# Layer 1 beside attention in halves of a product, row sums joined with 1e-9 by a reduce, and one raw-weight buffer given up for one more gated output

## The chip, the cores and the metric

One Trainium2 chip, one core of it. The metric is the device time of the kernel in microseconds (us), lower is better. The core has five engines that run side by side: PE (TensorE, with its weight loads shown as PEld), DVE (VectorE), ACT (ScalarE), POOL (GpSimd) and SP (SyncE, which here only issues transfers). Each runs its own list of instructions in order and waits on semaphores of the others.

## The reference

Attention with a mask by blocks of 64, for 4 batches, 8 heads, 576 positions and 64 features, then two feed-forward layers over 2304 tokens (512 features, 2048 hidden). All in float32.

```python
scores = scale * q @ k.T                       # 576 x 576 a head
scores = where(block_i >= block_j, scores, -1e9)
attn = exp(scores - max); attn /= attn.sum(-1) + 1e-9
x = (attn @ v) as 2304 x 512
h = x @ w_in;  g = max(h, 0) + alpha * min(h, 0);  x = g @ w_out        # layer 1
h = x @ w_in2; g = where(h > 0, h, exp(min(h, 0)) - 1); out = g @ w_out2  # layer 2
```

## The kernel before

**Precision.** Matrix products run in a reduced float32 with each factor split into a high and a low part, three products for one (`PASSES`). So whatever PE multiplies is first split on another engine: `copy` (L82 to L90) makes the high part, `low_part` (L78) the rest. Weights arrive as raw 64-bit floats, 512 KB a piece, and are turned into words and then split by `load_w` (L110): a transfer into a raw buffer (`wraw`, 3 buffers), two ACT operations (L127, L128), three DVE operations (L132, L133, L137), a POOL add (L142), an ACT copy (L151) and a DVE subtraction (L83, into `w`). A raw buffer is in use from the issue of its transfer until the POOL add. There are 64 such pieces, 32 a layer.

**Attention** goes by slots. A slot scores one tile of rows of a pair of heads. The first 16 slots (EARLY) are the first 256 rows of each of the 16 pairs; then come three slots a pair, i = 2, 3, 4. In a slot PE makes scores into one of two score buffers in PSUM (`twin`, ring `s`), DVE masks by memset (L299, L304) and takes the maximum (L296), ACT takes the exponential with its row sum (L324), two slots later DVE adds 1e-9 (L329) and inverts (L330) the sum and POOL scales the rows (L90), then PE transposes them (L352 to L369), and later multiplies by v (L413). Since two score buffers alternate, scores of a slot wait for the exponentials of the slot two before. Splits of q and k for later pairs (`split_q`, `split_k`) lie mostly on POOL.

**Layer 1 beside attention.** With only hidden units 0 to 511 (`FA` = 4 tiles of 128), layer 1 is computed for three units of 512 tokens as soon as their attention rows exist (`l1_beside`). A unit has 8 parts: four products into hidden tiles (L536, 12 matmuls of 512 columns each, then a gate on ACT, DVE, ACT and POOL) and four products into partial outputs (L557, 12 matmuls, then a copy to `z` that goes to DRAM). A loop in the main program puts a part on PE, then some slots, then a part. All parts use one PSUM bank (ring `h` is bank 7 alone). The order of every engine up to here is that of the code.

**The rest** (from 301 us on) runs steps: a hidden tile of a unit (12 matmuls), then two steps later the output of it (12 matmuls, L628 in layer 1, L603 in layer 2). Units A, B and D are layer 1, C is layer 2; A is 16 steps, 8 with 512 tokens and 8 with 256, B is three units of 4 steps. Here only PE's order is the code's; the other engines' lists, SP's too, are put in order ahead of time by a scheduler that works with its own estimates. It may start transfers and splits of weights long before their step, as soon as a raw buffer is free in its plan. Outputs of gates go to `gs_tile` (4 buffers `gs`, 3 buffers `gsl`).

## Time and profile before

| what | value |
|---|---|
| median of 3 runs | 1059.77 us (1059.53 to 1062.9) |
| the profiled execution | 1062.1 us, its span 1060.0 us |
| PE busy | 983.2 us, 93% of the span |
| DVE busy | 579.2 us, 55% |
| ACT, POOL busy | 442.8 us (42%), 358.7 us (34%) |
| mean granted clock of PE | 0.975 of 2.4 GHz |

The span is counted from the first to the last instruction; 2.1 us of the profiled execution lie outside of it. The busy shares are means over stretches that differ: beside attention all four compute engines are in use, in the last third PE alone is full.

### The profile page before, as it was taken

Reading aid. Unit: us, or ns where it says so; the run is one execution under the profiler, and the core shown is the slowest. Engines: PE = TensorE matmul, PEld = TensorE weight load, DVE = VectorE, ACT = ScalarE, POOL = GpSimd, SP = SyncE. Lnnn points to the kernel's source line nnn. Section 1 sums busy time; section 2 is a strip of 40 time slices with the busy share of each in tenths; the row PEclk is TensorE's granted clock in tenths of the full one; section 3 lists DMA queues with packets and bytes.
Section 4 is the critical chain, followed back from the end, with each engine's and each line's share of the span. In section 5 each row is a group of like instructions: output and inputs, shape, how many; then the busy total and the mean of one; then the engine's idle time right before and its main releaser. Section 6 shows DMA issues by size and latency. Waiting matters only on the chain.

```text
span 1060.0 us, 14175 instructions
## 1 busy us (share of the span) xinstructions
PE 983.2 (93%) x5072; PEld 790.7 (75%) x5072; DVE 579.2 (55%) x1047; ACT 442.8 (42%) x986; POOL 358.7 (34%) x410
## 2 busy tenths in 40 slices
PE   4888988998798799999999998899999999999997
PEld 3555765666577677878988887688888888888897
DVE  6886587677648995483313189833333333333343
ACT  4675566666635663353323255422222222222222
POOL 6876566667426663353323254200000000000000
PEclk9888999999999899999999999899999999999999
DMA  6451533353544767563526255200200300110010
GB/s 185 135 183 41 194 110 115 103 171 97 172 150 145 252 235 240 160 205 112 167 75 197 81 179 218 80 1 10 110 0 1 119 1 1 40 41 1 1 40 20
DMA packets 61157, 116.27 MB, mean 110 GB/s; under 512 B 11552, under 2 KB 29984, under 8 KB 59936
## 3 DMA queue, kind: packets, MB, share of 16 engines
q1 hardware_dynamic: 60800, 115.11, 32.8%
q8 instruction: 40, 0.66, 0.3%
q14 instruction: 29, 0.24, 0.1%
q10 hardware_dynamic: 288, 0.26, 0.1%
HBM read 83.89 MB, written 31.46 MB: 109 GB/s over the span
## 4 chain that ended last, share of the span: by engine, by line
PE 66%; DVE 16%; issue 5%; DMA 4%; POOL 4%; ACT 3%; SPq 1%; POOLq 0%; DVEq 0%; ACTq 0%
PE bank L603 18%; PE bank L578 18%; PE bank L536 10%; PE bank L628 9%; PE bank L413 4%; DVE w L83 4%; DVE wword L137 3%; DMA wraw<-w 3%; PE bank L557 2%; DVE wword L133 2%; DVE wword L132 2%; PE bank L359 2%; PE pair L279 2%; POOL p L90 1%; POOL wword L142 1%
## 5 line engine op out<-in xcount | busy, mean ns | idle before, releaser
L536 PE MATMUL bank<-x,w 128*128 128x512 f32 (+1 forms) x960 | 216.3, 376 | 2.2 <-DVE xtail L83 1.3
L578 PE MATMUL bank<-x,w 128*128 128x512 f32 (+1 forms) x960 | 211.4, 369 | 0.0
L536 PEld LDWEIGHTS bank<-x,w 128*128 128x128 f32 x960 | 171.1, 193 | 33.6 <-ACT xtail L419 1.4
L578 PEld LDWEIGHTS bank<-x,w 128*128 128x128 f32 x960 | 170.4, 190 | 31.7
L583 DVE TENSOR_SCALAR e<-e 128x512 f32<-128x512 f32 (+1 forms) x80 | 33.1, 414 | 181.3 <-ACT e L582 181.3
L603 PE MATMUL bank<-w,gs 128*128 128x512 f32 x498 | 123.1, 394 | 3.1 <-DVE z L639 2.1
L582 ACT ACTIVATE e<-bank 128x512 f32<-128x512 f32 (+1 forms) x80 | 44.4, 554 | 194.3 <-PE bank L578 194.3
L519 DVE SCALAR_TENSOR_TENSOR g<-neg,beta,bank 128x512 f32<-128x512 f32 (+1 forms) x80 | 55.1, 689 | 117.6 <-ACT neg L516 117.6
L142 POOL TENSOR_TENSOR wword<-wword,wraw 128x512 int32<-128x512 int32 x64 | 88.8, 1389 | 81.3 <-DVE wword L137 30.2
L603 PEld LDWEIGHTS bank<-w,gs 128*128 128x128 f32 x498 | 93.3, 189 | 23.8 <-DVE z L639 3.2
L628 PE MATMUL bank<-gs,w 128*128 128x512 f32 (+1 forms) x480 | 105.0, 366 | 4.8 <-POOL gs L83 2.6
L83 POOL TENSOR_TENSOR gs<-g,gs 128x512 fp32r<-128x512 f32 (+1 forms) x52 | 65.2, 1253 | 118.4 <-ACT gs L523 118.1
L628 PEld LDWEIGHTS bank<-gs,w 128*128 128x128 f32 x480 | 83.4, 190 | 20.7 <-POOL gs L83 3.4
L90 POOL TENSOR_SCALAR p<-p,stat 128x128 f32<-128x128 f32 (+4 forms) x144 | 84.2, 599 | 42.5 <-DVE stat L330 26.5
L324 ACT ACTIVATE p<-pair,stat 128x128 f32<-128x128 f32 (+4 forms) x144 | 78.2, 555 | 34.3 <-DVE stat L296 33.9
L603 PE MATMUL bank<-w,gsl 128*128 128x512 f32 x366 | 88.7, 390 | 0.0
L628 PE MATMUL bank<-gsl,w 128*128 128x512 f32 (+1 forms) x336 | 77.1, 377 | 11.1 <-POOL gsl L83 6.6
L516 ACT ACTIVATE neg<-bank 128x512 f32<-128x512 f32 (+1 forms) x80 | 44.0, 550 | 95.0 <-PE bank L536 94.9
L603 PEld LDWEIGHTS bank<-w,gsl 128*128 128x128 f32 x366 | 68.3, 188 | 13.8
L628 PEld LDWEIGHTS bank<-gsl,w 128*128 128x128 f32 x336 | 59.8, 193 | 24.3 <-POOL gsl L83 7.9
L83 DVE TENSOR_TENSOR w<-wword,w 128x512 fp32r<-128x512 f32 x64 | 68.7, 1091 | 14.2 <-ACT w L151 13.7
L296 DVE TENSOR_REDUCE stat<-pair 128x2 f32<-128x256 f32 (+3 forms) x80 | 63.1, 805 | 6.9 <-PE pair L285 4.8
(81 smaller groups left out, 1277.2 us busy)
## 6 DMA issues: line engine op xcount, KB each, us to landing
wraw<-w SPq DMA_DIRECT2D x64, 512.0 KB, 4.4
x<-xd SPq DMA_DIRECT2D x24, 512.0 KB, 7.4
xd<-x SPq DMA_DIRECT2D x4, 2048.0 KB, 6.7
x<-yd SPq DMA_DIRECT2D x4, 2048.0 KB, 8.0
vraw<-v_a SPq DMA_DIRECT2D x24, 256.0 KB, 4.5
zd<-z SPq DMA_DIRECT2D x20, 256.0 KB, 3.4
kraw<-kT SPq DMA_DIRECT2D x16, 288.0 KB, 3.2
yd<-gs SPq DMA_DIRECT2D x8, 512.0 KB, 4.9
```

Source lines behind the costliest of these rows:

```text
L83: return {"v": dve, "p": pool_e}[eng].tensor_tensor(out=out, in0=x, in1=f32(high), op=ALU.subtract)
L90: return pool_e.tensor_scalar(out, x, 1.0 if scale is None else scale, 1.0, ALU.mult, ALU.mult)
L142: pool_e.tensor_tensor(out=w, in0=w, in1=units, op=ALU.add)
L296: peak = lambda out, x, axis=AX.X: dve.tensor_reduce(out=out, in_=x, axis=axis, op=ALU.max, negate=True)
L324: act.activation(out=out, in_=x, func=AF.Exp, bias=stat[:, k:k + 1], accum_out=stat[:, w + k:w + k + 1])
L516: act.activation(out=neg, in_=h, func=AF.Relu, scale=-1.0)
L519: dve.scalar_tensor_tensor(out=g, in0=neg, scalar=beta[:, f:f + 1], in1=h, op0=ALU.mult, op1=ALU.add)
L536: pe.matmul(h, w_in(0, f, wp_, kc), x[:, xp_, kc, :n], start=kc == 0 and t == 0, stop=kc == KC - 1 and t == 2)
L578: pe.matmul(h, w_in(1, f, wp_, kc), x[:, xp_, kc, :], start=kc == 0 and t == 0, stop=kc == KC - 1 and t == 2)
L582: act.activation(out=e, in_=h, func=AF.Exp)
L603: pe.matmul(acc, gs[:, gp_, tg * P:(tg + 1) * P], w_out(1, f, wp_, 0, DM), start=f == 0 and t == 0, stop=f == NF - 1 and t == 2)
L628: pe.matmul(acc, w_out(0, f, wp_, m * P, P), gs[:, gp_, :n], start=first and t == 0, stop=last and t == 2)
```

## The change

Six edits:
- `l1_beside` puts half a product (6 matmuls) on PE at a time, 16 parts a unit instead of 8, over the same slots (10 for unit 0, 24 for units 1 and 2). The rule that deals out the slots is the same: after each part, the slots left over the parts left, rounded up.
- The high part of every early q goes to ACT instead of POOL (7 operations; the first one was on ACT before).
- The two masks of an early slot are one memset.
- Row sums go to every second column of a `stat` tile whose other columns hold 1e-9; the sum with 1e-9 is a DVE reduce over pairs instead of an add (`tensor_scalar`), and the inverse is taken in place. The six `stat` tiles are fixed and set once on POOL at the start.
- Two raw-weight buffers (and two word buffers) instead of three.
- Gated outputs alternate between 4 `gs` and 4 `gsl` buffers, instead of 4 and 3.

```diff
-    wraw_p = ctx.enter_context(pool("wraw", 3))
+    wraw_p = ctx.enter_context(pool("wraw", 2))
...
-            copy("a" if c.start == 0 and n == 0 else "p", qh, q[:, c], 0.125)
+            copy("a" if c.start == 0 else "p", qh, q[:, c], 0.125)
...
+    stats = [ap1.tile([P, 16], F32, name=f"stat{i}") for i in range(6)]
+    for t in stats:
+        pool_e.memset(t, 1e-9)
...
-            for t, lo, hi in EARLY_TILES:
-                dve.memset(sb[:64, :, hi - 64:hi], NEG)
+            dve.memset(sb[:64].rearrange("p x (t c) -> p x t c", t=2)[:, :, :, 64:P], NEG)
...
-        dve.tensor_scalar(stat[:, 2 * w:3 * w], stat[:, w:2 * w], 1e-9, None, ALU.add)
-        dve.reciprocal(stat[:, 3 * w:4 * w], stat[:, 2 * w:3 * w])
+        total = stat[:, TOTALS:TOTALS + w]
+        dve.tensor_reduce(out=total, in_=stat[:, SUMS:SUMS + 2 * w].rearrange("p (k t) -> p k t", t=2),
+                          axis=AX.X, op=ALU.add)
+        dve.reciprocal(total, total)
...
-        if late_pools and turn[0] % 7 % 2:
-            return late_pools[0].tile([P, 2, 512], F32R, tag="gsl", name="gsl", bufs=3)
+        if late_pools and turn[0] % 2:
+            return late_pools[0].tile([P, 2, 512], F32R, tag="gsl", name="gsl", bufs=4)
...
         for f in range(FA):
-            h = l1_h(u, f)
-            gs[f] = l1_gate(f, h, n, True)
-            end_tick()
-            yield
+            h = bank[take("h")][:, :n]
+            for part in halves:
+                for kc in part:
+                    for t, (wp_, xp_) in enumerate(PASSES):
+                        pe.matmul(h, w_in(0, f, wp_, kc), x[:, xp_, kc, :n],
+                                  start=kc == 0 and t == 0, stop=kc == KC - 1 and t == 2)
+                if part is halves[1]:
+                    gs[f] = l1_gate(f, h, n, True)
+                    end_tick()
+                yield
...
-            parts, n = l1_beside(u), FA + KC
+            parts, n = l1_beside(u), 2 * (FA + KC)
```

Three places show what this does to the lists.

PE, units 1 and 2 beside attention. Before, one cycle of three slots (`L279` 128x512 is the score of i = 3, `L285` of i = 4, `L279` 128x384 of i = 2 of the next pair; `p` rows are transposes, `vraw` rows the products with v):

```order
L536 MATMUL bank_106<-x_869,w 128x512 x12
L279 MATMUL pair_101<-kh,qh 128x512 x2
...
L365 MATMUL bank_104<-ident,p_1294 128x128 x4
...
L285 MATMUL pair_102<-kh,qdiag_117 128x288
...
L359 MATMUL bank_104<-ident,p_1345 128x128 x3
L279 MATMUL pair_101<-kh,qh 128x384 x2
...
L413 MATMUL bank_105<-pt,vraw_114 64x320 x6
...
L359 MATMUL bank_104<-ident,p_1388 128x128 x4
L536 MATMUL bank_106<-x_869,w 128x512 x12
```

The same engine, the cycle after the change:

```order
L562 MATMUL bank_106<-x_838,w 128x512 x6
L279 MATMUL pair_102<-kh,qh 128x512 x2
...
L373 MATMUL bank_105<-ident,p_1378 128x128 x4
...
L285 MATMUL pair_101<-kh,qdiag_115 128x288
...
L367 MATMUL bank_105<-ident,p_1444 128x128 x3
L562 MATMUL bank_106<-x_838,w 128x512 x6
L279 MATMUL pair_102<-kh,qh 128x384 x2
```

Six of twelve matmuls stay where the twelve were, and six now stand ahead of the scores of i = 2. In this part of a unit (its first 16 slots) six matmuls come every two slots, in the last 8 slots of a unit every slot.

PE, the end of unit 0, after the change:

```order
L573 MATMUL bank_106<-gs,w 128x512 x6
L279 MATMUL pair_101<-kh,qh 128x384 x2
...
L367 MATMUL bank_105<-ident,p_1077 128x128 x4
L573 MATMUL bank_106<-gs,w 128x512 x36
L562 MATMUL bank_106<-x_838,w 128x512 x6
```

Unit 0 has 10 slots for 16 parts, so its last six parts follow each other with no slot between; before, each part had one or two slots behind it.

DVE, unit A (gates are `g<-neg,beta,bank`, the rest are weights). Before, from the fourth gate to the fifth:

```order
L519 SCALAR_TENSOR_TENSOR g<-neg,beta,bank_3229 128x512
L83 TENSOR_TENSOR w<-wword,w 128x512 x3
L132 TENSOR_SCALAR wword<-wword 128x512
L133 TENSOR_SCALAR wword<-wword 128x512
L137 SCALAR_TENSOR_TENSOR wword<-wraw,wword 128x512
L132 TENSOR_SCALAR wword<-wword 128x512
L519 SCALAR_TENSOR_TENSOR g<-neg,beta,bank_3230 128x512
```

After:

```order
L527 SCALAR_TENSOR_TENSOR g<-neg,beta,bank_3161 128x512
L132 TENSOR_SCALAR wword<-wword 128x512
L133 TENSOR_SCALAR wword<-wword 128x512
L137 SCALAR_TENSOR_TENSOR wword<-wraw,wword 128x512
L83 TENSOR_TENSOR w<-wword,w 128x512
L527 SCALAR_TENSOR_TENSOR g<-neg,beta,bank_3162 128x512
```

Seven weight operations between two gates have become four here; over the first 18 gates (the 16 of A and two of B) there were 87, and there are 66. The other 21 stand later in the list, among the gates of B and D.

SP, unit A (`L117` is a raw weight piece, `x<-xd` the input of the next unit, for B's three units in turn). Before:

```order
L117 DMA wraw<-w 128x1024 x9
L501 DMA x_3556<-xd_83 128x2x512 x4
L117 DMA wraw<-w 128x1024 x3
...
L117 DMA wraw<-w 128x1024 x6
L501 DMA x_3879<-xd_84 128x2x512 x4
```

After:

```order
L117 DMA wraw<-w 128x1024 x8
L509 DMA x_3488<-xd_83 128x2x512 x4
L117 DMA wraw<-w 128x1024 x2
...
L117 DMA wraw<-w 128x1024 x4
L509 DMA x_3811<-xd_84 128x2x512 x4
```

The input of B's second unit stands behind 14 weight pieces where it stood behind 18.

## Rows read from the trace of the kernel before

**Rows 1.** Busy time by stage: engine busy (instructions), granted clock, DMA share, GB/s.

```profile
0.00:58.00 58.00, 37.73 (x275) 26.93 (x276) 44.48 (x108) 35.04 (x123) 44.26 (x75) 0.94 0.51 156
58.00:118.00 60.00, 51.80 (x293) 37.22 (x294) 40.38 (x95) 34.47 (x104) 39.24 (x62) 0.89 0.40 143
118.00:301.40 183.40, 159.40 (x1052) 112.58 (x1050) 130.77 (x300) 114.67 (x298) 110.72 (x152) 0.96 0.42 130
301.40:402.00 100.60, 88.80 (x453) 75.20 (x454) 87.69 (x116) 59.20 (x111) 56.52 (x40) 0.95 0.58 199
...
640.00:690.00 50.00, 44.16 (x177) 34.22 (x176) 43.55 (x59) 23.92 (x42) 18.87 (x13) 0.93 0.39 147
```

**Rows 2.** Groups by shape, 0 to 110 us: busy, mean ns, idle before.

```profile
L329 DVE TENSOR_SCALAR stat<-stat 128x4 f32<-128x4 f32 x16 | 7.2, 452 | 0.0
L296 DVE TENSOR_REDUCE stat<-pair 128x2 f32<-128x256 f32 x16 | 6.8, 424 | 0.5
...
L299 DVE MEMSET pair<- 64x128 f32 x32 | 5.3, 165 | 1.8
...
L90 POOL TENSOR_SCALAR qh<-qraw 128x512 fp32r<-128x512 f32 x7 | 4.7, 678 | 4.5 <-DMA qraw<-qT 3.9 <-PE pair L279 0.6
...
L89 DVE COPY z<-bank 128x512 f32<-128x512 f32 x1 | 0.7, 692 | 2.1 <-PE bank L557 2.1
...
L87 ACT ACTIVATE qh<-qraw 128x512 fp32r<-128x512 f32 x1 | 0.6, 629 | 1.2 <-DMA qraw<-qT 1.2
```

**Rows 3.** Line L329 alone: duration ns minimum/median/maximum, first and last start.

```profile
L329 DVE TENSOR_SCALAR stat<-stat x64: 139/156/1270, 17.1 to 287.1; 128x2 f32<-128x2 f32 x32, 128x4 f32<-128x4 f32 x16, 128x1 f32<-128x1 f32 x16
```

**Rows 4.** Waits of PE's weight loads, 0 to 110 us: total us, times, longest.

```profile
PEld bank L352 <- POOL p L90: 13.4, 18, 2.9
```

**Rows 5.** Timeline of PE: start us, duration, [idle before].

```profile
125.14 0.45 PE L279 MATMUL pair<-kh,qh 64*128 64x384 f32 x2 [1.03 <-issue]
...
242.04 0.45 PE L279 MATMUL pair<-kh,qh 64*128 64x384 f32 x2 [2.02 <-DVE stat L330]
...
254.78 0.44 PE L279 MATMUL pair<-kh,qh 64*128 64x384 f32 x2 [1.08 <-issue]
...
265.76 0.45 PE L279 MATMUL pair<-kh,qh 64*128 64x384 f32 x2 [1.02 <-issue]
...
402.84 2.88 PE L536 MATMUL bank<-x,w 128*128 128x512 f32 x12
```

**Rows 6.** Timeline of all engines, just ahead of the score at 254.78 us.

```profile
254.48 0.20 ACT L324 ACTIVATION_READ_ACCUMULATOR p<-pair,stat 128x1 f32 x1
```

**Rows 7.** The chain that ended last: start us, duration, what.

```profile
420.27 2.72 PE bank L536 x12
```

**Rows 8.** DVE's groups by line, 301.4 to 402 us.

```profile
L83 DVE TENSOR_TENSOR w<-wword,w 128x512 fp32r<-128x512 f32 x24 | 28.7, 1206 | 5.2 <-ACT w L151 4.7
L133 DVE TENSOR_SCALAR wword<-wword 128x512 uint32<-128x512 uint32 x23 | 18.8, 815 | 0.5
L132 DVE TENSOR_SCALAR wword<-wword 128x512 f32<-128x512 f32 x23 | 16.3, 713 | 1.3 <-ACT wword L127 1.3
L137 DVE SCALAR_TENSOR_TENSOR wword<-wraw,wword 128x512 uint32<-128x512 uint32 x23 | 16.2, 706 | 0.2
```

**Rows 9.** Timeline of SP's issues, 301 to 402 us (merged runs, waits within them included).

```profile
319.30 27.16 SPq L117 DMA_DIRECT2D wraw<-w  x9
346.51 2.98 SPq L501 DMA_DIRECT2D x<-xd  x4
...
364.73 17.44 SPq L117 DMA_DIRECT2D wraw<-w  x6
382.26 3.19 SPq L501 DMA_DIRECT2D x<-xd  x4
```

**Rows 10.** The page's DMA issues: count, KB each, median us to landing.

```profile
wraw<-w SPq DMA_DIRECT2D x64, 512.0 KB, 4.4
x<-xd SPq DMA_DIRECT2D x24, 512.0 KB, 7.4
```

More of the change, by code (lines that the diff above doesn't have):

```diff
@@ L286, in scores @@
                               start=t == 0, stop=t == 2)
+    MAXIMA, SUMS, TOTALS = 0, 4, 12
+    stats = [ap1.tile([P, 16], F32, name=f"stat{i}") for i in range(6)]
+    for t in stats:
+        pool_e.memset(t, 1e-9)
     def width(i):
@@ L293, in maxima @@
         s = st[n]
-        s["stat", i] = stat = ap2.tile([P, 16], F32, tag="stat", name="stat", bufs=6)
+        s["stat", i] = stat = stats[AT[n, i] % len(stats)]
         sb = s["sb", i]
@@ L310, in exponentials @@
         s = st[n]
-        stat, sb, w = s["stat", i], s.pop(("sb", i)), width(i)
+        stat, sb = s["stat", i], s.pop(("sb", i))
         tag = 2 + n % 3 if i == EARLY else i
@@ L323, in exponentials @@
         for k, (out, x) in enumerate(todo):
-            act.activation(out=out, in_=x, func=AF.Exp, bias=stat[:, k:k + 1], accum_out=stat[:, w + k:w + k + 1])
+            act.activation(out=out, in_=x, func=AF.Exp, bias=stat[:, k:k + 1],
+                           accum_out=stat[:, SUMS + 2 * k:SUMS + 2 * k + 1])
     def normalise(n, i):
@@ L328, in normalise @@
         stat, w = s.pop(("stat", i)), width(i)
-        dve.tensor_scalar(stat[:, 2 * w:3 * w], stat[:, w:2 * w], 1e-9, None, ALU.add)
-        dve.reciprocal(stat[:, 3 * w:4 * w], stat[:, 2 * w:3 * w])
+        total = stat[:, TOTALS:TOTALS + w]
+        dve.tensor_reduce(out=total, in_=stat[:, SUMS:SUMS + 2 * w].rearrange("p (k t) -> p k t", t=2),
+                          axis=AX.X, op=ALU.add)
+        dve.reciprocal(total, total)
         for k, t in enumerate(s.pop(("w", i))):
-            copy("p", t, t, stat[:, 3 * w + k:3 * w + k + 1])
+            copy("p", t, t, total[:, k:k + 1])
     def place(half, j):
@@ L545, in l1_beside @@
     def l1_beside(u):
-        n, gs = UNITS[u], {}
+        n, x, gs = UNITS[u], x1[u], {}
+        halves = ((0, 1), (2, 3))
         for f in range(FA):
-            h = l1_h(u, f)
-            gs[f] = l1_gate(f, h, n, True)
-            end_tick()
-            yield
+            h = bank[take("h")][:, :n]
[8 more added lines that the diff above has]
+                yield
         for m in range(KC):
             acc = bank[take("h")][:, :n]
-            for f in range(FA):
-                for t, (wp_, gp_) in enumerate(PASSES):
-                    pe.matmul(acc, w_out(0, f, wp_, m * P, P), gs[f][:, gp_, :n],
-                              start=f == 0 and t == 0, stop=f == FA - 1 and t == 2)
-            to_z(u, m, acc)
-            end_tick()
-            yield
+            for part in halves:
+                for f in part:
+                    for t, (wp_, gp_) in enumerate(PASSES):
+                        pe.matmul(acc, w_out(0, f, wp_, m * P, P), gs[f][:, gp_, :n],
+                                  start=f == 0 and t == 0, stop=f == FA - 1 and t == 2)
+                if part is halves[1]:
+                    to_z(u, m, acc)
+                    end_tick()
+                yield
     def z_tile(m):
```

## The prediction

> **What bounds the kernel now.** I read the busy time by stage first [rows 1]. Up to 58 us attention runs alone: POOL is busy 44.3 of 58 us and DVE 44.5, PE only 37.7. From 58 to 118 us unit 0 of layer 1 runs beside it, and from 118 to 301.4 us units 1 and 2: PE is busy 159.4 of 183.4 us there, DVE 130.8, ACT 114.7, POOL 110.7. From 301.4 to 402 us DVE is busy 87.7 of 100.6 us and PE 88.8. From 640 to 690 us, where layer 1 gives way to layer 2, PE is busy 44.2 of 50. Elsewhere PE is nearly full, and nothing in the change touches its work. So what can be won lies in PE's idle time before 402 us and in the clock: the granted clock is 0.94, 0.89, 0.96 and 0.95 in these four stages. A granted 0.96 is a mean of the levels 1.2 and 2.4 GHz, so PE stood at the lower one for 8% of 183.4 us, 15 us, and what it computed there took twice its time.
>
> Then the waits. Early, PE's transposes wait for POOL's scaled rows: 13.4 us over 18 waits [rows 4]. In units 1 and 2 there is one wait in each cycle of three slots, ahead of the scores of i = 2. Thirteen such rows stand from 125.14 to 265.76 us, so a cycle takes 140.6/12 = 11.72 us; the idle time is 1.03 us in the first, 2.02 in one and 1.02 in the last [rows 5]. Releasers given there as "issue" are read by time: ACT's second sum of i = 3 ends at 254.68 us [rows 6], and the score starts at 254.78. So PE waits for the exponentials that empty the score buffer. The cycle from 254.78 to 265.76 us took 10.98 us with 1.02 idle: 9.96 us of PE's work.
>
> **First 58 us.** Six of the seven moved high parts of q fall here. POOL loses 6 x 0.678 = 4.1 us; ACT gets 6 x 0.629 = 3.8 us [rows 2] and stands at 35.0 of 58 [rows 1]. What waits behind such an ACT operation is the copy out of the transposes and the slot's exponentials, which wait for DVE's maximum anyway. DVE: two memsets of 0.165 us become one of twice the size, between 0.165 and 0.33; I take 0.25, a gain of 0.08 a slot. The add takes 0.452 us in the mean [rows 2], but 0.139 at least and 1.27 at most [rows 3]: it is not its work that takes long, it waits for something. The reduce has no row of its own size. It lies between 0.139 us (the shortest add) and 0.424 (the smallest reduce that there is, 256 columns from PSUM); with 8 columns it is nearer to the first, I take 0.17. Over 13 slots DVE so gains 13 x (0.28 + 0.08) = 4.7 us.
>
> The Trainium skill ("SBUF — State Buffer", on which operations grab the pair of ports shared with GpSimd) says that `tensor_scalar` can block against GpSimd and that a `tensor_reduce` never does on trn2. The spread of rows 3 agrees; that the reduce is free of it, no row here shows. Against it stands "VectorE: DVE Perf Modes", rules for kernel authors, which calls `tensor_reduce` the slowest operation of that engine: if so, at 0.424 us, the edit would gain 0.03 us a slot.
>
> DVE and POOL are links of one chain, so the two gains do not add up: 4 us, between -4 (ACT's 3.8 us all in the way) and 9.
>
> **58 to 118 us, unit 0.** Its 96 matmuls are the same, at 2.72 us for 12 [rows 7] 21.8 us. Halves fill smaller gaps, and the relief above goes on for three slots. But the last six parts come in one run. All use one bank, so after each of three products PE waits for the copy of 0.692 us [rows 2] and its handover: 3 x 0.9 = 2.7 us lost. And with one slot between parts the gate must have read the bank by the next slot's part: up to three waits of some 0.7 us too, 2.1 us. I take a gain of 3 us; between -5 (the two losses and no gain) and 10 (about what PE's idle 60 - 51.8 = 8.2 us and part of its lower clock allow).
>
> **118 to 301.4 us, units 1 and 2.** In the first 16 slots of a unit six matmuls come every two slots, 9 a cycle instead of 12: PE's work is 9.96 - 3 x 0.227 = 9.28 us a cycle, and one of the two halves, 1.36 us, always stands between the scores of i = 3 and of i = 2, where PE idles 1 to 2 us. DVE's 130.8 us over 16 cycles are 8.2 us a cycle, so it would be 88% busy, and a cycle can't be expected to come down to PE's work. Between 9.28 and today's 10.98 I take two thirds of the way, 10.4. There are 2 x 16/3 = 10.7 of these: 111 us. The last 8 slots of unit 1 have 18 matmuls a cycle: 9.96 + 6 x 0.227 = 11.3 us with PE full, 2.7 cycles, 30 us. The last 8 of unit 2 are the drain of attention: today 183.4 - 13.33 x 11.72 = 27 us with 32 matmuls (7.3 us); with 48 (10.9 us) and some 3 us of waits filled, 28 us. Sum 169, a gain of 14 us. With cycles of 10.98 it would be 8, with 9.28 26.
>
> **301.4 to 402 us, unit A and B's first.** All of this would take PE, at 2.72 us for 12 matmuls of 512 columns and half for 256, 62.6 us to B's first product and 19.0 more to the fifth, which makes 383; it started at 402.84 [rows 5]. 20 us are lost, because DVE's 93 weight operations take 80.0 us there [rows 8], 0.86 each, and gates stand behind them. With two raw buffers 21 of them come after: 18 us of DVE's time. What takes the limit over is SP. In front of the input of B's second unit stand 14 weight pieces. Today 9 and 6 pieces took 27.2 and 17.4 us [rows 9], 3.0 each, so a piece held one of three buffers for some 9 us; with two that is 4.5 us a piece. From 319.3 us: 14 x 4.5 + 3 (the four inputs between) + 7.4 to landing [rows 10] = 393. So the product at 402.84 starts at 394 at the earliest: 9 us, between 0 and 20. B's third unit comes four pieces later, 18 us against PE's 21.8 for a unit, and the last weights of A and B are needed only by D, behind B's three units.
>
> **640 to 690 us.** The same spreading of weights on DVE, 43.6 of 50 us busy: 1 us, between -2 and 4. The eighth gated buffer: no row has PE waiting for a free one; 0.
>
> **Sum.** 4 + 3 + 14 + 9 + 1 = 31 us. The profiled execution took 1062.1 us (span 1060.0, 2.1 around it), 2.3 above the median of the three runs; 1062.1 - 31 = 1031, and since a median lies a little lower, 1030. Its own range, by halves of the bounds: 1018 to 1043.
>
> **Rivals.**
> - *Part of it.* DVE and POOL hold the cycle, light cycles stay at 10.98 us (8 us), unit 0 gives nothing, SP leaves 4 us: 3 + 0 + 8 + 4 = 15, 1046 us. For it: both are 77% busy early [rows 1] and in turn wait on each other. Against: PE's wait has one named place and a half now stands there. Chance 0.20.
> - *The clock.* With 9 matmuls a cycle PE works less in a row; if the granted clock in units 1 and 2 fell from 0.96 to the 0.89 of the stretch before [rows 1], 14% more of 169 us at the lower level cost half of that, 12 us: 1042 us. The Trainium skill ("TensorE: Matmul & The Clock Gate", what is actually happening) says that idling lets the clock drop and activity brings it back; it would speak for this rival only if the gaps grew, and here they shrink. Chance 0.08.
> - *Slower: raw buffers.* If a piece holds its buffer for R us, the input of B's second unit lands at 319.3 + 3 + 14 R/2 + 7.4, and the start at 402.84 moves by 7R - 73. With the other terms at 22 us this decides from R = 13.6 us on; at R = 15.5 the loss is 35 us, the sum -13, 1073 us. For it: waits of SP for POOL's add are already in its list, and the DMA share is 0.58 there [rows 1]. Against: R is 9 us today, with more pieces in flight. Chance 0.07.
> - *No change* (gains early given back as waits later): 1060 us, 0.05.
> - *More*: light cycles near PE's work and A's full 20 us: 1008 us, 0.08.
>
> The forecast has the remaining 0.52. A measurement here tells about 0.3%, 3 us. Faster 0.88 (forecast, part, clock, more), same 0.05, slower 0.07. The range 1012 to 1050 leaves out most of the last three cases.
>
> **What would show it.** In the profile after: cycles of 10.4 us with under 0.5 us of idle ahead of the 128x384 scores, granted clock near 0.98 in that stretch; L329's successor near 0.17 us with no long ones; B's fifth product 20 to 45 us earlier, of which 9 to unit A, with the weight operations on DVE under 65 us in A; SP's runs of weight pieces at 4.5 us each, and PE perhaps waiting for `x<-xd`. It would be wrong if light cycles stay at 11 us, if the run of 36 matmuls shows waits above 3 us, or if a piece holds its buffer for 13 us or more.

## The result and the profile after

The changed kernel takes 1045.36 us (median of 4 runs, 1044.22 to 1052.43), where before took 1061.34 in the runs beside it: a ratio of 0.9874, 95% interval 0.985 to 0.9897. It is faster by 16 us (1.3%, clear of noise), about half of the 31 that were forecast. Its profiled execution has a span of 1043.1 us, 16.9 below before's, at a mean granted clock of 0.981.

The stages, by the kernel's own limits: 0 to 58 us, unit 0, units 1 and 2, A to the fifth product of B, and 50 us from layer 2's first product on. They answer to [rows 1].

```profile
core 0: us, PE busy (x) PEld busy (x) DVE busy (x) ACT busy (x) POOL busy (x), PEclk, DMA share, GB/s
0.00:58.00 58.00, 38.16 (x272) 27.57 (x274) 41.57 (x100) 39.98 (x136) 39.02 (x75) 0.94 0.52 158
58.00:120.00 62.00, 49.53 (x300) 34.65 (x296) 37.94 (x89) 34.63 (x100) 40.41 (x61) 0.94 0.42 145
120.00:290.30 170.30, 157.94 (x1049) 111.86 (x1049) 120.56 (x296) 110.98 (x290) 110.70 (x149) 0.97 0.43 130
290.30:388.40 98.10, 88.47 (x456) 75.33 (x457) 67.41 (x97) 50.67 (x96) 49.02 (x37) 0.97 0.54 186
634.00:684.00 50.00, 47.90 (x201) 38.05 (x200) 41.38 (x64) 27.11 (x47) 19.16 (x13) 0.97 0.43 158
```

Where the 16.9 us come from is read from the starts of the same PE instructions in both traces (one profiled execution each):

| stage (from one start to the next) | before | after | gain | forecast |
|---|---|---|---|---|
| start to unit 0's first product | 60.31 | 59.83 | 0.5 | 4 |
| unit 0, to unit 1's first product (118.06; 120.09) | 57.75 | 60.26 | -2.5 | 3 |
| units 1 and 2, to A (301.40; 290.29) | 183.34 | 170.20 | 13.1 | 14 |
| A, to B's fifth product (402.84; 388.42) | 101.44 | 98.13 | 3.3 | 9 |
| on to layer 2's first product (645.51; 634.08) | 242.67 | 245.66 | -3.0 | 0 |
| layer 2, to the end | 414.5 | 409.0 | 5.5 | 1 |

One term out of six is right. Three are too high, one of them in sign too, a loss on the way to layer 2 was not foreseen, and layer 2 itself gave more than was forecast.

**Units 1 and 2.** In the whole stretch PE's timeline shows idle time ahead of a 128x384 score only twice, where before it stood ahead of thirteen [rows 5]:

```profile
135.88 0.44 PE L279 MATMUL pair<-kh,qh 64*128 64x384 f32 x2 [1.16 <-issue]
...
157.19 0.69 PE L279 MATMUL pair<-kh,qh 64*128 64x384 f32 x2 [2.45 <-ACT p L329]
```

PE's waits in the whole stretch fell from 22.6 to 11.4 us. The five cycles from 203.27 to 255.72 us, in unit 2, take 52.45/5 = 10.5 us each in the mean, though singly 8.5 to 14.4; 10.4 was forecast.

**Unit 0.** PE's timeline has the gate's waits, once per hidden tile, and the waits of the last run for copies (0.78, 0.72, 0.78; the last is read by time, since DVE's copy to `z` at 119.35 us ends at 120.04):

```profile
70.30 1.66 PE L562 MATMUL bank<-x,w 128*128 128x512 f32 x6 [1.15 <-DVE g L527]
...
82.75 2.93 PE L562 MATMUL bank<-x,w 128*128 128x512 f32 x6 [4.54 <-DVE g L527]
...
94.89 1.66 PE L562 MATMUL bank<-x,w 128*128 128x512 f32 x6 [1.60 <-DVE g L527]
...
102.79 1.66 PE L573 MATMUL bank<-gs,w 128*128 128x512 f32 x6 [1.43 <-DVE g L527]
...
112.56 3.02 PE L573 MATMUL bank<-gs,w 128*128 128x512 f32 x12 [0.78 <-DVE z L89]
116.30 3.01 PE L573 MATMUL bank<-gs,w 128*128 128x512 f32 x12 [0.72 <-ACT z L87]
120.09 1.66 PE L562 MATMUL bank<-x,w 128*128 128x512 f32 x6 [0.78 <-DVE stat L336]
```

The gate waits sum to 8.7 us. DVE's timeline ahead of the longest shows why it is long: the gate (L527) starts at 81.95 us and takes 0.74, and in front of it in DVE's list stand the operations on a piece of weights (with a wait for ACT) and the next slot's statistics.

```profile
78.39 0.87 DVE L132 TENSOR_SCALAR wword<-wword 128x512 f32<-128x512 f32 x1 [1.03 <-ACT wword L127]
...
79.89 0.69 DVE L137 SCALAR_TENSOR_TENSOR wword<-wraw,wword 128x512 uint32<-128x512 uint32 x1
80.49 0.15 DVE L336 TENSOR_REDUCE stat<-stat 128x4 f32<-128x8 f32 x1
...
81.08 0.96 DVE L302 TENSOR_REDUCE stat<-pair 128x2 f32<-128x768 f32 x1
81.95 0.74 DVE L527 SCALAR_TENSOR_TENSOR g<-neg,beta,bank 128x512 f32<-128x512 f32 x1
```

**Units A and B.** DVE's weight operations fell from 93 that took 80.0 us to 74 that took 57.5 (19.6 + 16.0 + 11.6 + 10.3 in the groups that answer to [rows 8]), yet PE still stops. SP's runs of weight pieces, which answer to [rows 9]:

```profile
307.16 28.92 SPq L117 DMA_DIRECT2D wraw<-w  x8
...
341.12 4.65 SPq L117 DMA_DIRECT2D wraw<-w  x2
...
355.46 11.43 SPq L117 DMA_DIRECT2D wraw<-w  x4
367.63 2.49 SPq L509 DMA_DIRECT2D x<-xd  x4
```

The runs of the 14 pieces sum to 45.0 us, but SP also waits between them: from the first piece to the input of B's second unit, issued at 367.63 us, it is 60.5 us, near the 66 of the prediction (14 x 4.5 + 3). That input had landed at 377.96 us, 10 us before its product at 388.42. So the product did not wait for it. PE's and ACT's waits say what held it. ACT's wait for landing pieces, from A's first product to B's fifth, before and then after:

```profile
ACT wword L127 <- DMA wraw<-w: 3.4, 4, 2.1
```

```profile
ACT wword L127 <- DMA wraw<-w: 14.4, 9, 3.8
```

The longest of these, in ACT's timeline, has the copy of a finished sum to `z` behind it, and PE needs that bank:

```profile
345.96 0.38 ACT L524 ACTIVATE neg<-bank 128x256 f32<-128x256 f32 x1
350.11 0.66 ACT L127 ACTIVATE wword<-wraw 128x512 f32<-128x512 f32 x1 [3.77 <-DMA wraw<-w]
350.68 0.57 ACT L87 COPY z<-bank 128x512 f32<-128x512 f32 x1
```

```profile
351.30 2.34 PE L645 MATMUL bank<-gsl,w 128*128 128x256 f32 x9 [3.57 <-ACT z L87]
```

PE waits 10.8 us in this stretch (13.0 before): this once for a copy, else mainly for gated outputs. ACT also waits 16.7 us for POOL's add (9.0 before). The chain that ended last, which the profile follows back from the last instruction, ties these together. From 302 to 365 us it runs round the two raw buffers: POOL's add (L142) frees one, the next piece is issued into it and lands, and ACT, DVE and POOL turn it into words (start us, duration, what):

```profile
318.51 3.60 DMA wraw<-w
322.19 0.67 ACT wword L127
...
325.52 1.31 POOL wword L142
326.84 3.21 DMA wraw<-w
...
341.12 8.97 DMA wraw<-w
350.11 0.67 ACT wword L127
```

Transfers of pieces make up 29.6% of that chain from A to B's fifth product, where before they made up 9.1% and DVE's weight operations 34%. The transfer of 8.97 us, behind the longest wait above, was issued 3 us after the four input transfers of B's first unit, the last of which landed at 348.87 us; the piece after it took 5.9, the twelve others up to B's second input 3.1 to 4.3.

**Start of layer 2.** Where before had 5.8 us of waits and a stretch at the lower clock (granted 0.93, [rows 1]), two waits ahead of the first output are left:

```profile
649.61 0.96 PE L620 MATMUL bank<-w,gsl 128*128 128x512 f32 x3 [1.09 <-DVE z L656]
651.41 2.85 PE L620 MATMUL bank<-w,gsl 128*128 128x512 f32 x6 [0.84 <-DVE zl L656]
```

### The profile page after: what moved, and what is told of

Its sections match the earlier page's. It is cut to its first block, busy times and chain, and to the rows that moved or that the text cites. A ratio compares the mean times of both kernels' runs of the same rounds, so it can differ in the third digit from the quotient of the medians.

```text
span 1043.1 us, 14146 instructions
## 1 busy us (share of the span) xinstructions
PE 978.9 (94%) x5072; PEld 787.6 (76%) x5072; DVE 549.2 (53%) x1031; ACT 445.6 (43%) x993; POOL 356.2 (34%) x409
## 4 chain that ended last, share of the span: by engine, by line
PE 66%; DVE 13%; DMA 7%; POOL 5%; issue 4%; ACT 4%; SPq 0%; POOLq 0%; ACTq 0%; DVEq 0%
PE bank L620 18%; PE bank L595 17%; PE bank L645 9%; PE bank L544 8%; DMA wraw<-w 5%; PE bank L421 4%; PE bank L573 3%; POOL wword L142 3%; PE bank L562 2%; PE pair L279 2%; DVE wword L132 2%; DVE wword L137 2%; DVE wword L133 2%; PE bank L367 2%; DVE w L83 1%
## 5 line engine op out<-in xcount | busy, mean ns | idle before, releaser
L595 PE MATMUL bank<-x,w 128*128 128x512 f32 (+1 forms) x960 | 210.6, 368 | 0.0
L595 PEld LDWEIGHTS bank<-x,w 128*128 128x128 f32 x960 | 169.9, 189 | 31.5
L544 PE MATMUL bank<-x,w 128*128 128x512 f32 (+1 forms) x816 | 176.2, 366 | 1.3 <-DVE xtail L83 1.3
L544 PEld LDWEIGHTS bank<-x,w 128*128 128x128 f32 x816 | 142.3, 190 | 26.0 <-ACT xtail L427 1.4
L142 POOL TENSOR_TENSOR wword<-wword,wraw 128x512 int32<-128x512 int32 x64 | 92.1, 1442 | 81.3 <-DVE wword L137 45.4
L620 PE MATMUL bank<-w,gsl 128*128 128x512 f32 x432 | 106.7, 394 | 2.1 <-DVE z L656 1.1
L527 DVE SCALAR_TENSOR_TENSOR g<-neg,beta,bank 128x512 f32<-128x512 f32 (+1 forms) x80 | 55.1, 689 | 99.7 <-ACT neg L524 99.6
L645 PE MATMUL bank<-gsl,w 128*128 128x512 f32 (+1 forms) x408 | 93.6, 378 | 11.9 <-POOL gsl L83 4.7
L620 PE MATMUL bank<-w,gs 128*128 128x512 f32 x432 | 104.8, 390 | 0.0
L620 PEld LDWEIGHTS bank<-w,gsl 128*128 128x128 f32 x432 | 80.8, 189 | 20.1 <-DVE z L656 2.0
L645 PEld LDWEIGHTS bank<-gsl,w 128*128 128x128 f32 x408 | 73.1, 196 | 27.2 <-POOL gsl L83 5.7
L620 PEld LDWEIGHTS bank<-w,gs 128*128 128x128 f32 x432 | 80.5, 188 | 16.6 <-DVE gs L83 0.3
L329 ACT ACTIVATE p<-pair,stat 128x128 f32<-128x128 f32 (+4 forms) x144 | 78.2, 555 | 25.5 <-DVE stat L302 23.5
L645 PE MATMUL bank<-gs,w 128*128 128x512 f32 (+1 forms) x408 | 88.9, 365 | 0.2
L645 PEld LDWEIGHTS bank<-gs,w 128*128 128x128 f32 x408 | 70.5, 189 | 13.6 <-POOL gs L83 1.5
L83 DVE TENSOR_TENSOR w<-wword,w 128x512 fp32r<-128x512 f32 x64 | 57.5, 903 | 30.9 <-ACT w L151 28.1
```

The lines of the kernel that those rows point to most:

```text
L83: return {"v": dve, "p": pool_e}[eng].tensor_tensor(out=out, in0=x, in1=f32(high), op=ALU.subtract)
L142: pool_e.tensor_tensor(out=w, in0=w, in1=units, op=ALU.add)
L329: act.activation(out=out, in_=x, func=AF.Exp, bias=stat[:, k:k + 1], accum_out=stat[:, SUMS + 2 * k:SUMS + 2 * k + 1])
L527: dve.scalar_tensor_tensor(out=g, in0=neg, scalar=beta[:, f:f + 1], in1=h, op0=ALU.mult, op1=ALU.add)
L544: pe.matmul(h, w_in(0, f, wp_, kc), x[:, xp_, kc, :n], start=kc == 0 and t == 0, stop=kc == KC - 1 and t == 2)
L595: pe.matmul(h, w_in(1, f, wp_, kc), x[:, xp_, kc, :], start=kc == 0 and t == 0, stop=kc == KC - 1 and t == 2)
```

## Experiments

The theory at the start: each part of the change acts in its own stretch, the halves win in units 1 and 2 and lose in unit 0, and in A the two buffers turn a limit of DVE into waits of ACT. The main rival: the relief on DVE, not the halves, won units 1 and 2. Starts in us, from one profiled execution of each kernel; "layer 2" is the start of its first product, and "layer 2 to end" the span less that start. Ratios are to the kernel before in the runs beside each.

| run | unit 0 | A | layer 2 | A to layer 2 | layer 2 to end | ratio (95%) |
|---|---|---|---|---|---|---|
| before | 60.31 | 301.40 | 645.5 | 344.1 | 414.5 | 1 |
| changed | 59.83 | 290.29 | 634.1 | 343.8 | 409.0 | 0.9874 (0.985 to 0.9897) |
| halves alone | 60.31 | 297.39 | 642.2 | 344.8 | 414.4 | 0.9973 (0.9949 to 0.9997) |
| small edits alone | 57.64 | 291.60 | 635.9 | 344.3 | 414.5 | 0.9941 (0.991 to 0.9972) |
| two buffers alone | 61.35 | 299.69 | 641.6 | 341.9 | 409.6 | 0.9915 (0.989 to 0.9941) |
| unit 0 whole | 57.63 | 282.86 | 629.3 | 346.4 | 409.8 | 0.9816 (0.9757 to 0.9875) |
| two banks | 60.56 | 289.87 | 635.0 | 345.2 | 409.5 | 0.9874 (0.9858 to 0.9891) |
| add, not reduce | 59.42 | 291.93 | 633.4 | 341.4 | 409.5 | 0.9868 (0.9848 to 0.9888) |
| q on POOL | 59.77 | 293.20 | 636.4 | 343.2 | 410.0 | 0.9878 (0.986 to 0.9897) |
| program order | 58.99 | 287.00 | 622.9 | 335.9 | 419.8 | 0.9855 (0.984 to 0.987) |
| parts first | 59.51 | 287.20 | 622.2 | 335.0 | 416.5 | 0.9798 (0.9777 to 0.9818) |
| fast pieces | 59.14 | 287.21 | 657.3 | 370.1 | 420.0 | 1.0178 (1.0155 to 1.0201) |
| together | 58.67 | 282.69 | 615.3 | 332.6 | 416.4 | 0.9764 (0.9744 to 0.9785) |
| together, three buffers | 58.85 | 281.40 | 615.4 | 334.0 | 408.0 | 0.9663 (0.9641 to 0.9685) |
| changed, three buffers | 57.70 | 288.45 | 634.6 | 346.2 | 416.1 | 0.9944 (0.9923 to 0.9965) |
| changed, three words | 57.91 | 292.86 | 636.9 | 344.0 | 409.4 | 0.9891 (0.9863 to 0.9919) |
| together, three words | 58.65 | 283.58 | 616.4 | 332.8 | 408.4 | 0.9684 (0.9662 to 0.9705) |
| together, two words | 58.70 | 282.27 | 616.1 | 333.8 | 416.3 | 0.9756 (0.9731 to 0.9782) |

How far single profiles of one program differ can be read here. The changed kernel, and the two below that differ from it only in the number of buffers (three raw buffers, three words), have the same program up to A: unit 0 takes 60.3, 59.5 and 63.2 us in them, unit 1 starts at 120.1, 117.2 and 121.1, and A at 290.3, 288.5 and 292.9. A difference of 2 to 4 us at one of these points shows nothing by itself.

**The parts, each alone.** Halves alone is `before` with the new `l1_beside` and `n = 2 * (FA + KC)`.

> Kernel before with layer 1's products beside attention in halves, nothing else. Theory (each part acts in its own stretch): units 1 and 2 are shorter by 8 to 13 us, because a half stands in the gap ahead of the 128x384 scores; unit 0 is longer by 3 to 6 us, because PE waits for the gate to leave the one bank 7 (8.7 us in the changed kernel) with no relief on DVE and POOL to pay for it; first 58 us and the raw weights as before. Together 1052 to 1057 us. Rival 1 (the gain of units 1 and 2 comes from the relief on DVE, not from the halves): units 1 and 2 shorter by under 4 us, 1060 or more. Rival 2 (what is won is waited for again in unit A, where DVE's weight operations are the limit): A starts 8 us earlier, the fifth product of B does not, 1060.

It took 1058.04 us. Units 1 and 2 took 173.75 us (gain 9.6), unit 0 63.33 (loss 5.6, with 9.3 us of waits for the gate). The theory holds at both places, though the time lies 1 us above its range. Rival 1 falls, and so does rival 2: B's fifth product comes 4.4 us earlier, A 4.0.

Small edits alone is the changed kernel with the whole products and the three buffers of before.

> Kernel before with the small edits alone: fixed statistics tiles, sum by pairs, one memset for two, high part of q on ACT; whole products, three raw buffers. Theory (each part in its own stretch): first 58 us shorter by 0.5 us as in the changed kernel, unit 0 by 2 to 4 (the relief without the waits for bank 7), units 1 and 2 by 1 to 3; 1053 to 1057 us. Rival (units 1 and 2 gain by the relief on DVE): 13 us there, 1045 us. Rival (relief off the path everywhere): 1060 us.

It took 1053.86 us. Unit 0 took 53.08 us (gain 4.7), units 1 and 2 180.88 (gain 2.5). So the relief pays in unit 0 (how much is read below from more kernels), and the halves make most of the gain in units 1 and 2: 9.6 of 13.1 us, where the 2.5 of the small edits is within what single profiles differ by. The first product came 2.7 us earlier, not 0.5; that is taken up below.

Two buffers alone:

```
-    wraw_p = ctx.enter_context(pool("wraw", 3))
+    wraw_p = ctx.enter_context(pool("wraw", 2))
-        if late_pools and turn[0] % 7 % 2:
-            return late_pools[0].tile([P, 2, 512], F32R, tag="gsl", name="gsl", bufs=3)
+        if late_pools and turn[0] % 2:
+            return late_pools[0].tile([P, 2, 512], F32R, tag="gsl", name="gsl", bufs=4)
```

> Kernel before with two buffers of raw weights and eight of gated outputs, nothing else. Theory (with two buffers ACT waits for pieces to land, with z copies and gates behind it in its queue, and this takes back most of what DVE wins): nothing before unit A, ACT's waits for landing pieces up from 3.4 to over 10 us until B's fifth product, which comes 2 to 4 us earlier; the start of layer 2 gives another 3 to 5; 1053 to 1057 us. Rival (the forecast's SP arithmetic): fifth product 9 us earlier, 1050 us. Rival (the two buffers cost): 1063 us or more.

It took 1052.46 us, a little under the range. B's fifth product came 397.29 - 299.69 = 97.6 us after A, 3.8 less than before, with 12.6 us of ACT's waits for landing pieces; layer 2 is 4.9 us shorter. The theory holds; the 9 us that the forecast drew from SP's arithmetic do not come. Transfers of pieces are 33.8% of the chain here too.

**Unit 0: the gate's bank.** Whole products in unit 0 only:

```
-        halves = ((0, 1), (2, 3))
+        halves = (range(4),) if u == 0 else ((0, 1), (2, 3))
-            parts, n = l1_beside(u), 2 * (FA + KC)
+            parts, n = l1_beside(u), (FA + KC) * (1 if u == 0 else 2)
```

> Changed kernel with unit 0 of layer 1 in whole products (eight parts over its ten slots), units 1 and 2 in halves as before. Theory (unit 0's loss is PE waiting for the one bank 7, first for the gate, 8.7 us, then in the last run for the copies, 2.3 us): these waits fall under 3 us, unit 1 starts 4 to 6 us earlier than in the changed kernel, and so does the end: 1039 to 1041 us. Rival (POOL and DVE set the slots of unit 0, PE's waits only show the slack): the waits come back ahead of transposes and scores, 1045 us.

It took 1042.05 us, 3 less than the changed kernel and 1 above the range; its interval is wide and reaches the changed kernel's ratio, so the time alone does not show the gain. Unit 0 took 53.55 us in place of 60.26, and it takes 53.6 to 55.9 in the five kernels that add halves in units 1 and 2 alone, where it takes 59.5 to 63.3 in all that have halves in unit 0 on one bank. PE's list of waits in it holds 0.7 us for the gate, where the changed kernel has 8.7:

```profile
PE bank L421 <- DVE x L83: 3.3, 2, 2.1
PE bank L360 <- POOL p L90: 2.4, 1, 2.4
PE bank L562 <- ACT pt L87: 0.9, 1, 0.9
PE bank L573 <- DVE g L527: 0.7, 1, 0.7
```

A starts 7.4 us earlier. B's fifth product comes 92.4 us after it, 5.8 less than in the changed kernel, but the way on to layer 2 takes 8.4 more, so 2.6 of the 7.4 are given back. To tell the bank from the halves:

```
-        ring("t", 4, 5, 6)
-        ring("h", 7)
+        ring("t", 4, 5)
+        ring("h", 6, 7)
```

> Changed kernel, halves in unit 0 too, but layer 1 has two banks beside attention (6 and 7) and the transposes and second products two (4, 5) in place of three. Theory (unit 0 lost because one bank must be read by the gate before the next slot's half): PE's waits for the gate fall from 8.7 us to under 2, unit 1 starts 5 to 8 us earlier than at 120.1, and as with whole products in unit 0 about half of that reaches the end: 1041 to 1043 us. Rival (the halves' spacing costs, not the bank): unit 1 starts at 118 or later, 1044 us or more. Rival (two banks are too few for attention): new waits of over 10 us of PE ahead of transposes and second products, 1055 us or more.

This kernel leaves out a wait that attention needs: with two banks for three, a slot's last transposes overwrite its second product before that is copied out, so its output is not the reference's, and a kernel with that wait may be slower. PE's work is the same, so the run can tell about the gate's waits. The gate's waits are gone altogether, unit 1 starts at 115.30, 4.8 us earlier, and unit 0 takes 54.7 us: it was the one bank. But PE now waits 5.7 us for DVE's copies out of the banks of the transposes in unit 0, and A starts only 0.4 us earlier, so nothing is left at the end (1047.38 us, the changed kernel's ratio). The theory is right on the cause and wrong on the total (1041 to 1043).

**The small edits apart.** The add again, on the new tiles (`tensor_scalar(total, sums, 1e-9, None, ALU.add)`):

> Changed kernel, but the sum and 1e-9 are joined by an add of a constant on DVE again, in place of the sum by pairs; tiles, memset and q as changed. Theory (the add's time was waiting for POOL, not work): its mean is 0.40 to 0.50 us in the first 110 us again, with single ones over 1 us, where the sum by pairs has 0.15; unit 1 starts 1 to 4 us later than at 120.1, A 2 to 5 us later than at 290.3, and the end 2 to 4 us: 1047 to 1050 us. Rival (the relief is one memset and POOL's rid of q's high part): 1045 us.

The lines of the reduce in the changed kernel, and of the add here (min, median and max in ns):

```profile
L336 DVE TENSOR_REDUCE stat<-stat x64: 134/145/154, 17.6 to 273.6; 128x2 f32<-128x4 f32 x32, 128x4 f32<-128x8 f32 x16, 128x1 f32<-128x2 f32 x16
```

```profile
L337 DVE TENSOR_SCALAR stat<-stat x64: 134/160/1386, 17.4 to 275.7; 128x2 f32<-128x2 f32 x32, 128x4 f32<-128x4 f32 x16, 128x1 f32<-128x1 f32 x16
```

The long ones are back with the add, and only with it (mean of the 16 early ones 0.482 us). Unit 1 starts 2.0 us later and A 1.6, less than one program's profiles differ by, and the ratio is the changed kernel's (1047.54 us, 0.9868). So the reduce is shown to rid DVE of the long adds, but not to make the kernel faster.

q on POOL again for all but the first pair:

```
-            copy("a" if c.start == 0 else "p", qh, q[:, c], 0.125)
+            copy("a" if c.start == 0 and n == 0 else "p", qh, q[:, c], 0.125)
```

> Changed kernel, with the high part of q on POOL again for all but the first pair. Theory (on ACT it stands behind three operations on a piece of weights and ahead of the next slot's scores, which cancels what POOL wins): no wait of PE for q's high part on ACT, POOL 4 us busier in the first 58 us, the start of unit 0 within 1 us of 59.8: 1044 to 1047 us. Rival (POOL's relief carries the early gain): unit 0 starts 2 to 4 us later, 1047 to 1049 us. Rival (ACT's part costs more than POOL's relief gives): 1041 to 1043 us.

1048.7 us, ratio 0.9878: not to be told from the changed kernel by time. The first product starts at 59.77, as the theory says; unit 0 takes 62.8 us, 2.5 more, which is again within what profiles of one program differ by. What POOL's relief is worth is not shown.

**Units A and B: order or pace.** In program order every engine and SP keep the order of the code after attention, where the scheduler set all but PE's:

```
-    with tc.manual_schedule(engines={ET.PE}):
+    with tc.manual_schedule(engines={ET.PE, ET.Activation, ET.DVE, ET.Pool, ET.SP}):
```

> Changed kernel, but in the stage after attention all engines and SP's queue follow the order in which the code emits the work (w_at's places for the weights), where the scheduler chose it before. Theory (the scheduler's order puts the pieces of weights, which with two buffers land late, ahead of z copies and gates in ACT's queue, and these waits are what unit A and B keep losing): ACT's waits for landing pieces no longer have PE's next need behind them, from A's first product to layer 2's first it takes 328 to 336 us in place of 343.8, 1030 to 1038 us. Rival (the pieces come too slowly in any order): waits of PE for weights in D, 1045 to 1060 us.

A to layer 2 took 335.9 us, as the theory says; B's fifth product came 372.77 - 287.00 = 85.8 us after A in place of 98.1. PE's own products are 82% of the chain in this stretch and transfers of pieces 5.7%; but only 11 pieces are issued in it, where the changed kernel issues 18. The time is 1046.09 us all the same, since layer 2 took 10.8 us more. In DVE's timeline three operations on weights stand ahead of a gated output's low part, and PE waits for that part, ten times:

```profile
660.82 0.42 DVE L132 TENSOR_SCALAR wword<-wword 128x512 f32<-128x512 f32 x1
661.27 0.43 DVE L133 TENSOR_SCALAR wword<-wword 128x512 uint32<-128x512 uint32 x1
661.73 0.69 DVE L137 SCALAR_TENSOR_TENSOR wword<-wraw,wword 128x512 uint32<-128x512 uint32 x1
662.34 0.68 DVE L83 TENSOR_TENSOR gsl<-e,gsl 128x512 fp32r<-128x512 f32 x1
```

```profile
663.08 1.20 PE L620 MATMUL bank<-w,gsl 128*128 128x512 f32 x4 [0.97 <-DVE gsl L83]
```

So the parts go first, in front of what else is due at the tick:

```
+    def soon(emit):
+        due.setdefault(tick[0] + 1, []).insert(0, emit)
...
-            later(1, gate())
+            soon(gate())
...
-        later(1, parts)
+        soon(parts)
```

> Program order for all engines after attention, and each product's second step (rounding and low part of the gated output) is emitted ahead of the operations on weights of the same tick. Theory (in program order layer 2 loses ten times 0.97 us because the three bit operations on a piece of weights, 1.54 us, stand ahead of a gated output's low part in DVE's queue): these ten waits go, layer 2's first product to the end takes 409 to 411 us in place of 419.8, and A to layer 2 stays at 334 to 338 us; 1033 to 1036 us. Rival (DVE has no room there, the wait moves to the weights): PE's waits come back ahead of products with layer 2's weights, 1042 us or more.

1039.11 us: better by 7, but the term is only half right. The waits of 0.97 us fell to 0.2, and layer 2 still took 416.5 us. What holds it then is found below.

Program order also asks for pieces more slowly than the scheduler did, so the next run asks for them fast:

```
-            w_at[1 + i * 26 // 16] = 0, 8 + f, r
-            w_at[first_of["D", 2] + 1 + 2 * i] = 1, f, r
+            w_at[1 + i] = 0, 8 + f, r
+            w_at[17 + i if f < 4 else first_of["D", 2] + 1 + 2 * (i - 8)] = 1, f, r
```

> Program order for all engines after attention, with pieces of weights asked for at the pace that the scheduler had chosen: one a step from A's second step on, 24 in the first 25 steps, where program order had 15. It tells the order from the pace. Theory 1 (the order alone was at fault): A to layer 2 stays at 334 to 338 us, 1042 to 1045 us. Theory 2 (the pace: with two buffers pieces are asked for faster than they come, and any engine that works in order waits for them with PE's next need behind): ACT's waits for landing pieces rise to over 10 us again from A to B's fifth product, A to layer 2 takes 341 us or more, 1048 us or more.

1079.16 us, slower than before. A to layer 2 took 370.1 us. The longest of ACT's waits for landing pieces in ACT's timeline, with the gate behind it for which PE then waits:

```profile
351.25 0.66 ACT L127 ACTIVATE wword<-wraw 128x512 f32<-128x512 f32 x1 [8.85 <-DMA wraw<-w]
...
353.27 0.40 ACT L531 CAST gs<-g 128x256 fp32r<-128x256 f32 x1
```

```profile
353.73 0.58 PE L645 MATMUL bank<-gs,w 128*128 128x256 f32 x1 [5.49 <-ACT gs L531]
```

Theory 2 holds: the pace costs. Pieces are asked for faster than two buffers let them come, and ACT then waits in front of PE's next need, from A to B's fifth product 18.6 us for landing pieces and another 25.0 for words that DVE has not yet finished with. The piece behind the wait of 8.85 us again stands right behind four input transfers, the last of which landed at 347.90 us. At the fast pace the scheduler's order (343.8 us) is even better than the code's (370.1). The scheduler's order at the slow pace, and the code's at the fast pace with three words, were not run.

**All together, and which buffer.** Unit 0 whole, program order and parts first:

> The changed kernel with what the runs point to: unit 0 in whole products, program order after attention, gated outputs ahead of weights. Theory (the three gains lie in different stretches): A starts at 282 to 284 us, layer 2 at 618 to 621, span 1028 to 1031; 1029 to 1033 us. Rival (an earlier A meets weights that are late): A to layer 2 takes 340 us or more, 1035 us or more.

> The same as the run with all three together, but with three buffers of raw weights and seven of gated outputs. Theory (two buffers only help where the scheduler would ask for too much at once; in program order the pace is set by the code): within 3 us of that run. Rival 1 (a third buffer lets pieces land before ACT comes to them): 3 to 8 us faster. Rival 2 (two buffers spread DVE's work in any order): 4 to 9 us slower, at the start of layer 2.

Together with two buffers: 1035.61 us, above the range because layer 2 took 416.4 us again. With three buffers and seven gated outputs: 1024.7 us. That is 11 us faster, more than rival 1 says, and not for its reason: A to layer 2 is no shorter (334.0 us, 332.6 with two buffers), the gain is in layer 2 (408.0 us). The pool holds two tiles for a piece, the raw piece (L117) and the word made from it, so the change cut both. The last four runs take them apart, three buffers in the changed kernel first:

> Changed kernel with three buffers of raw weights and words and seven of gated outputs again: the undoing of that part in the changed kernel. Theory (the parts add up: two buffers give nothing before A, 0 to 2 us from A to layer 2's first product, 5 behind it): layer 2's first product to the end 413 to 416 us in place of 409.0, ACT's waits for landing pieces between A and B's fifth product back under 6 us, 1049 to 1053 us. Rival (with A earlier the two buffers matter more, or less): from A to layer 2 differs from 343.8 by over 4 us.

> Changed kernel with two buffers of raw pieces but three of the words made from them. Theory (with the scheduler's order the raw pieces alone pace the work, a piece's word is free before the next piece lands): 1043 to 1048 us, layer 2's first product to the end 408 to 411. Rival (the second word buffer is what spreads DVE's work at the start of layer 2): 413 us or more there, 1048 to 1051 us.

> The run with all three together, with two buffers of raw pieces, three of words and seven of gated outputs. Theory (in program order ACT waits 2.36 us a step for DVE's low part to leave one of two words, with layer 2's exponential behind it): these waits go, layer 2's first product to the end falls from 416.4 to 408 to 411 us, 1026 to 1030 us. Rival (the raw pieces pace it): 1033 us or more.

> The same with three buffers of raw pieces, two of words and seven of gated outputs. Theory (two words are what costs at the start of layer 2): layer 2's first product to the end stays at 414 to 418 us, 1032 to 1036 us. Rival (raw pieces): 1023 to 1027 us.

In program order it is the words: with three, layer 2 takes 408.4 us and the kernel 1025.91; with two 416.3 and 1033.79, whatever the raw pieces. ACT's list of waits from 616 to 720 us has the reason with two words, and with three it is gone:

```profile
ACT wword L130 <- DVE w L83: 25.7, 11, 2.4
```

In the scheduler's order it is the raw pieces: two of them shorten layer 2 from 416.1 us (changed, three buffers: 1055.51 us, above its range by 2.5) to 409.4, with three words or two (1047.5 us). In that kernel with three buffers ACT waited 5.9 us for pieces up to B's fifth product, 101.8 us after A (390.25 - 288.45).

## Why the prediction was wrong

**Units 1 and 2 (14 us, measured 13.1): right**, and for its reason. Halves alone gain 9.6 us there, the waits ahead of the 128x384 scores went from thirteen to two, the cycles are 10.5 us in the mean, the granted clock 0.97. Against the profile of two buffers alone (181.4 us there, the same program as before up to A) the gain is 11.2 us, so the size is good to some 2 us. The clock's rival falls with it.

**Unit 0 (3 us, measured -2.5): mis-sized, even in sign.** The mechanism was named: the single bank and the last run. The run cost 2.3 us, 2.7 forecast. The gate was put at "up to three waits of some 0.7 us", 2.1 us; it is four waits, 8.7 us. The step priced the gate's own work and left out its place in DVE's list: it stands behind the next slot's maximum, and in slots with weights behind the three operations on a piece, which in turn wait for ACT. The relief that was to pay for it is some 3 us: with whole products unit 0 takes 53.1 to 55.9 us in the six kernels that have the small edits, 57.7 and 56.9 in the two that do not.

**First 58 us (4 us, measured 0.5).** One profile does not tell this size. The program up to there is the same, but for the number of raw buffers, in the changed kernel and 11 of the runs (two banks, the add and q on POOL are left out), and unit 0's first product starts there between 57.63 and 59.83 us, 58.6 in the mean; in the three kernels with before's first stretch it is 60.31, 60.31 and 61.35. The gain is about 2 us, half of the term. The operations were priced rightly: the reduce takes 0.145 us (0.17 forecast), the memset 0.272 (0.25). All 64 reduces lie between 134 and 154 ns, beside adds of up to 1386. The Trainium skill ("SBUF — State Buffer", who interferes with whom) has a reduce as free of the ports shared with GpSimd on trn2, and these durations agree. The Trainium skill ("VectorE: DVE Perf Modes", rules for kernel authors) calls a reduce the slowest operation of its engine; at this size it is not (median 0.145 us, 0.160 for the add). So DVE's work did shrink; PE's waits did not in this profile (only those of its weight loads for POOL's rows fell, from 9.7 to 7.9 us). Up to 58 us, before and then after:

```profile
PE pair L279 <- ACT p L324: 8.2, 5, 4.7
PE bank L352 <- POOL p L90: 4.1, 3, 2.6
```

```profile
PE pair L279 <- ACT p L329: 8.7, 5, 4.8
PE bank L360 <- POOL p L90: 5.4, 3, 2.5
```

The prediction let DVE's and POOL's gains through to PE and did not show that PE's waits end on them.

**A to B's fifth product (9 us, measured 3.3): the step that failed.** "What takes the limit over is SP" was the reading, and the only thing seen to wait for SP was the input of B's second unit. The first half held: some 20 fewer weight operations stand in the stretch. SP's sum came near too, though not for its reason: the 9 us for which a piece holds its buffer were read from merged runs, and from issue to POOL's add it is 11.8 us before and 9.1 after, in the median. But the bound was taken for the start. The input was there 10 us early, and the same loop round two buffers held PE elsewhere: ACT works in order, and gates and copies to `z` stand in its list behind pieces that land late (14.4 us of waits, 3.4 before) and behind POOL's add (16.7, 9.0 before). The chain runs round that loop until 365 us. At a slower pace, in the code's order, 85.8 us are reached, close to PE's own 81.6; how much of that is pace and how much order stays open. The prediction named what waits for SP and did not ask the same of ACT.

**On to layer 2 (0 us, measured -3.0).** The same waits of ACT go on in B, where the sums into `z` on DVE stand behind operations on weights: PE waits 2.4 us there, and 0.91 of the clock is granted in the 20 us around it. Not foreseen.

**Layer 2 (1 us, measured 5.5): mis-sized to the other side.** Two raw buffers spread the pieces away from its start: in its first 20 us DVE's weight operations take 17.8 us with three, 10.4 to 11.0 with two, in the scheduler's order. All kernels with three raw buffers in the scheduler's order take 414.4 to 416.1 us, all with two 409.0 to 410.0.

**Eighth gated buffer (0).** Never tried alone; no PE wait for a free one was read.

In all, 13.1 of 14 us came in units 1 and 2, where the argument went from one named wait of PE to what the edit puts in its place, and 3.8 of 17 in the rest. The number lies at the "part of it" rival (1046 us). That rival had unit 0 at nothing and SP at 4 us, which is near; its main reason, light cycles of 10.98 us, is not what happened, so its hit is in part luck.

## What to carry over

When an operation is moved or a buffer cut, read for each engine in order what stands in its list in front of the operation that PE needs next; a gate of 0.74 us cost 4.5 where weights stood ahead of it. A prefetch that is asked for faster than its buffers allow can cost more than a late one, since the engine that unpacks it waits in order: in the code's order and with two buffers the kernel took 1046 us at the slow pace and 1079 at the fast one. When a bound on one transfer has been worked out, look whether the chain that ended last passes through that transfer at all. Unit 0 in whole products, program order after attention, gated outputs ahead of weights and three buffers give 1024.7 us, 3.4% under before and about 2% under the changed kernel.

## What was not expected of the hardware

The same program reached unit 0's first product at 57.63 us in one kernel and at 59.83 in another, a spread as large as the gain looked for there; what makes it stays open. A weight piece of 512 KB that was issued right behind four transfers of a unit's input took 9.0 us to land, where most took 3.1 to 4.3, and ACT's longest wait for a piece stood there in the changed kernel and in the one with fast pieces alike. Of the 7.4 us that unit 0 in whole products wins ahead of A, 4 arrive at the end.
